# A planned one-core kernel: GpSimd is made to wait for the VectorE instruction listed ahead of it, TensorE's fillers change, the first-stage result gets a second buffer

## The chip, the core and the metric

One core of a Trainium2 chip runs the whole kernel. The metric is the time of one execution in device microseconds (us). The kernel before took 555.62 us, the median of three runs (557.21, 555.62 and 553.38 us).

## What is computed

An input of 2048 tokens by 576 channels goes through two residual blocks. Each block normalises the tokens and applies a scale and a shift that come from a small vector `c`. The first block is a state-space layer (a causal convolution of every channel over all tokens, with taps from 128 complex poles per channel). The second is a gated feed-forward network on the eight tokens with the highest router score; every other token passes unchanged.

```
mod = (silu(c) @ w_mod).reshape(1, 6, 1, 576)          # sa, ca, ga, sb, cb, gb
h = layernorm(x) * (1 + ca) + sa
x = x + ga * A(h)
h = layernorm(x) * (1 + cb) + sb
x = x + gb * B(h)

A: P = exp((A * dt)[:, :, None] * pos);  K = 2 * einsum("dn,dnl->dl", C, P).real
   y = irfft(rfft(h, 2L) * rfft(K, 2L))[:L] + h * D_skip
B: r = h @ w_r;  idx = the 8 tokens with the largest r
   y = (silu(h[idx] @ w_gate) * (h[idx] @ w_up)) @ w_down * sigmoid(r[idx])
   h + scatter(y, idx)
```

## The kernel before, in words

The program runs in four stages, which overlap.

**Preparation.** `mod_row` makes the six modulation rows from 1440 KB pieces of `w_mod` (TensorE, line 626, then line 640). `prep_polar` and `prep_poles` turn the pole parameters into 16-bit pieces on VectorE. `stage1(b)`, for eight pairs of token groups, multiplies the normalised tokens `hb` by a 32-point transform (lines 739 and 742). The result goes from PSUM into two SBUF tiles, `xs0` and `xs1` (line 748), and four DMAs on SyncE's queue write these to `dX` in DRAM (line 754). Both tiles have one buffer: the copies of `stage1(b+1)` wait until the stores of `stage1(b)` have landed.

**Taps and convolution.** For each of 36 blocks of 16 channels, `mags` makes exponentials `E` (ScalarE, line 798), `trig` makes sines and cosines `SC` (ScalarE, lines 828, 830, 832) after a range reduction `n` (VectorE, line 347), and `taps` multiplies them: `SC<-SC,E` on GpSimd, `Bc<-E,SC` and two products `E<-E,SC` on VectorE, one of these on either engine. TensorE contracts the products (line 858); the result goes to `ksb`. `kx` transforms the taps (line 879). When a group of eight blocks is done, `conv` runs eight steps: TensorE (lines 923 and 937), two products `t<-b,us` on VectorE, two sums `t<-t` on GpSimd, the inverse on TensorE (line 971), a DMA through `dZ`, and `y_group` (line 1009).

**The memory that is handed on.** The setup's tiles (tag `su`) must all be done before the convolution's pool `grp` opens (`swap3`). The pool for the feed-forward weights, `w1`, opens when the taps and the fourth group are done (`swap4`), a second one, `w2`, when the fifth is (`swap5`).

**Tail.** Router scores, selection, the feed-forward network on 32 rows, the normalised output (three VectorE passes `zr<-zr` of 1.35 us each per pair of token groups), and the scatter. The weights stream from DRAM in 39 DMAs.

**What sets the order.** No engine's order is written by hand. `Plan` holds 2254 operations with a cost, dependencies, ring buffers and PSUM banks, and lists them by start times of its own; `SEEDS` is a table of numbers that perturbs the priorities and so picks one list. Then `emit` issues the operations in the order of that list, each on its engine's queue. An operation marked `lock` (the GpSimd instructions and the VectorE instructions with two SBUF inputs or in a fast mode) is listed so that no two of them run at once: in the list, GpSimd and VectorE take turns. On the chip nothing enforces these turns. An instruction starts when its data are there and its engine's queue has reached it.

**Fillers.** `spare` counts gaps in TensorE's list, and `idle` puts 128x128 fp32 matmuls of the identity (part of `csm`, a 413 KB constant) into them, at line 438. Their result is not used. A gap gets no more of them than bring the last 3.4 us (`WINDOW`) to a share of 0.8 (`SHARE`). They come after 12 us of the planner's time (`FROM`), and stop from 130 us (`HOLD`) until the PSUM bank that they use is free again.

Of the kernel before, what the change touches and what calls it, by code (L numbers as in the profile page):

```python
# [37 lines left out]
class Plan:  # L38

    LAT = {"V": .12, "A": .17, "P": .12, "T": .21, "Q": 0.0, "X": 0.0}  # L40
    LOOK, TABLE, RATE, FLY, AHEAD = .3, 1.28, 370.0, 2.0, 2.0
    SEEDS = ((15, 0.32), (789, 1), (1215, 0.32), (1311, 0.32), (1887, 0.32), (3271, 0.32), (4311, 0.32), (5223, 0.32), (5319, 0.32), (13159, 0.32), (16055, 0.32), (23663, 0.32), (35487, 0.32), (35511, 0.32), (36455, 0.32), (37575, 0.32), (39311, 0.32), (43039, 0.32), (62487, 0.32), (94159, 0.32), (220535, 0.32), (314815, 0.32), (322255, 0.32), (349359, 0.32), (362815, 0.32))
    wide = False
# [163 lines left out]
    def spare(self):  # L207

        ts = [o for o in self.done if o.on == "T"]
        out, load = {}, []  # L210
        late = max((o.gone for o in self.done if o.need and set(o.names) & set(self.NARROW)), default=0.0)
        for a, b in zip(ts, ts[1:]):
            t0 = a.start + (a.cost["T"] if isinstance(a.cost, dict) else a.cost)
            t1 = b.start
            load.append((a.start, t0))
            while load and load[0][1] < t1 - self.WINDOW:
                load.pop(0)
            full = sum(y - max(x, t1 - self.WINDOW) for x, y in load)
            n = min(int((t1 - t0 - self.GAP) / self.UNIT), math.ceil((self.SHARE * self.WINDOW - full) / self.UNIT))
            if n > 0 and (t1 < self.HOLD or t0 > late) and t0 > self.FROM:  # L220
                out[b] = n
                load.append((t0, t0 + n * self.UNIT))
        return out

    GAP, WINDOW, UNIT, FROM, SHARE, idle = .3, 3.4, .27, 12.0, .8, None

    def emit(self):
        Plan.last = self
        self.done = self.schedule()
        fill = self.spare() if self.idle else {}  # L230
        for o in self.done:
            if o in fill:
                self.idle(fill[o], o.start > self.HOLD)
            if o.need:
                o.fn(o.on, o.names)
            else:
                o.fn(o.on)


# [101 lines left out]
def adaln_s4d_mod_kernel(ctx, tc, u, par0, par1, head, wm, wr, wg, wu, wd, cs, cfg, cmv, out):  # L341
    nc = tc.nc
    V, S, P, T, Q = nc.vector, nc.scalar, nc.gpsimd, nc.tensor, nc.sync
    AX = mybir.AxisListType.X

    def ts(o, a, s1, op0, s2=None, op1=None, eng=None):
        (eng or V).tensor_scalar(o, a, s1, s2, op0=op0, **({"op1": op1} if op1 is not None else {}))  # L347

    def stt(o, a, s, b, op0, op1, **kw):
        V.scalar_tensor_tensor(o, a, s, b, op0=op0, op1=op1, **kw)  # L350

    def tt(o, a, b, op, eng=None):
        (eng or V).tensor_tensor(o, a, b, op=op)  # L353

# [78 lines left out]
    def idle(n, late):  # L433

        if "p" not in IDLE or IDLE["late"] != late:
            IDLE["p"], IDLE["late"] = ps.tile([128, 128], F32, name=plan.NARROW[0]), late
        for _ in range(n):
            T.matmul(IDLE["p"], ident, ident, start=True, stop=True)  # L438
    plan.idle = idle
    CH = ((0, 128), (128, D - 128))  # L440
    PP, PAR = {0: pp}, {0: pp.tile([128, 4, 128], F32, name="par0")}
# [283 lines left out]
    def stage1(b):  # L725
        for m in range(2):
            ring(f"xs{m}", b, 1)
        for j in range(2):
            ln_rows(2 * b + j)
            for hh in range(2):  # L730
# [13 lines left out]
                for m in range(2):  # L744
                    def g(e, j=j, m=m, cs_=cs_, st=st):
                        if (b, m) not in XS:
                            XS[b, m] = su.tile([128, 2, D], F32, name=f"xs{m}")
                        CP[e](XS[b, m][:, 1 - j if m == 0 else j, cs_], st["p"][m])
                    op("AV", {"A": ac(288), "V": vc(288)}, g, uses=[mm], w=[("xsp", b, m, j, hh)], inst=[(f"xs{m}", b)],
                       tag="su")  # L750
        for m in range(2):
            s0 = 14 - 2 * b if m == 0 else 2 * b
            for cc in range(2):
                op("Q", .45, lambda e, m=m, cc=cc, s0=s0: Q.dma_start(
                    dX[cc, m, s0:s0 + 2].rearrange("s h k d -> (h k) s d"), XS[b, m][64 * cc:64 * cc + 64]),
                   r=[("xsp", b, m, j, hh) for j in range(2) for hh in range(2)], inst=[(f"xs{m}", b)],
                   w=[("dX", b, m, cc)], dma=295, tag="su")
# [636 lines left out]
    def cols(e, nm):  # L1394

        stc["p"] = banks([128, 2, 5], nm)[0]
        for i, x in enumerate((cb(), sb())):
            for k in range(5):
                for h in range(2):
                    c = 128 * k + 64 * h if k < 4 else 512  # L1400
                    T.matmul(stc["p"][64 * h:64 * h + 64, i, k:k + 1], x[0:1, c:c + 64], ones[0:1, 0:1],
                             start=True, stop=True, tile_position=(0, 64 * h))
    m_ = op("T", 1.2, cols, r=both("cb") + both("sb"), bank=1, tag="su")
    op("AV", {"A": .2, "V": .12}, lambda e: CP[e](csc, stc["p"]), uses=[m_], w=["csc"], tag="su")
# [69 lines left out]
```

## Time and profile before

| | |
|---|---|
| median of three runs | 555.62 us (553.38 to 557.21) |
| the profiled execution | 557.26 us, span 555.5 us |
| instructions | 17725 |
| busy time: TensorE matmuls, weight loads | 470.0 us (85% of the span), 330.4 us |
| busy time: VectorE, ScalarE, GpSimd | 410.5 us (74%), 322.6 us (58%), 171.7 us (31%) |
| fillers | 255 matmuls, recorded as 510 |
| HBM read, written | 71.88 MB, 23.62 MB |

The span runs from the program's first instruction to its last, and the execution's own time is 1.76 us longer. An fp32 matmul leaves two records. A busy time is a sum over the whole span, so it does not tell which engine bounds a stage; the chain of work that ended last does, step by step. PEclk is the share of the full clock that TensorE was granted.

### The profile page before, as it was taken

The page shows a single profiled execution, that of the slowest core. Times are in us where ns is not written, and L with a number is a line of the kernel's source. Part 1 is how long each engine was busy: PE and PEld are TensorE (multiplying, and loading weights), DVE is VectorE, ACT ScalarE, POOL GpSimd, SP SyncE. Part 2 cuts the span into 40 slices and gives each one's busy share as a digit, 9 for nine tenths or more (in the row PEclk, how much of TensorE's full clock was granted, in tenths as well). Part 3 has the DMA queues.
Part 4 walks back from the last instruction along what each step waited for, and adds up shares of the span by engine and source line. Part 5 has one row for each costly group of instructions (what it writes and reads, how often), then busy time and mean ns, then how long its engine had stood idle before and what let it go on. Part 6 is the DMA issues. An engine that isn't in the chain of part 4 may idle for free.

```text
span 555.5 us, 17725 instructions
## 1 busy us (share of the span) xinstructions
PE 470.0 (85%) x7589; PEld 330.4 (59%) x7589; DVE 410.5 (74%) x861; ACT 322.6 (58%) x529; POOL 171.7 (31%) x135
## 2 busy tenths in 40 slices
PE   3979898788877789999998899888889479989886
PEld 2755454553556556767676567566778366446453
DVE  4699889877644968798978999979877588554501
ACT  5488579656555879778896897876421003421100
POOL 0003124302212656366836465365722000000000
PEclk9999989887778979999999999999999996999988
DMA  8965333204392211373345323153387899899993
GB/s 349 426 274 173 105 98 88 73 25 128 100 322 90 59 40 61 102 184 100 95 126 146 94 81 99 58 153 117 109 238 200 199 295 383 258 280 379 389 320 144
DMA packets 67285, 96.66 MB, mean 174 GB/s; under 512 B 12891, under 2 KB 46811, under 8 KB 66054
## 3 DMA queue, kind: packets, MB, share of 16 engines
q1 hardware_dynamic: 66070, 92.49, 51.4%
q10 hardware_dynamic: 1104, 3.01, 1.4%
q8 instruction: 60, 0.98, 0.8%
q14 instruction: 19, 0.16, 0.1%
q0 software_dynamic: 32, 0.02, 0.0%
HBM read 71.88 MB, written 23.62 MB: 172 GB/s over the span
## 4 chain that ended last, share of the span: by engine, by line
PE 37%; DVE 22%; DMA 17%; issue 10%; ACT 9%; POOL 3%; SPq 2%; POOLq 0%; DVEq 0%; ACTq 0%
DMA out<-zr 6%; PE b L971 6%; PE b L858 4%; PE b L923 4%; PE b L937 4%; DVE zr L353 4%; DVE n L347 4%; DMA w<-in_wu 3%; PE b L739 3%; PE b L879 3%; DVE Bc L353 3%; DVE t L353 3%; ACT E L798 3%; DMA dX<-xs 2%; DVE E L350 2%
## 5 line engine op out<-in xcount | busy, mean ns | idle before, releaser
L353 POOL TENSOR_TENSOR SC<-SC,E 128x1024 f32<-128x1024 f32 x36 | 87.2, 2424 | 132.4 <-ACT SC L832 61.1
L353 POOL TENSOR_TENSOR t<-t 128x256 f32<-128x256 f32 (+1 forms) x80 | 68.7, 863 | 96.2 <-DVE t L353 94.3
L438 PEld LDWEIGHTS b<-csm 128*128 128x128 f32 x510 | 70.1, 210 | 18.8 <-issue 16.4
L438 PE MATMUL b<-csm 128*128 128x128 f32 x510 | 78.0, 303 | 0.0
L798 ACT ACTIVATE E<-b 128x512 f32<-128x512 f32 x108 | 57.8, 608 | 8.1 <-PE b L792 6.9
L353 DVE TENSOR_TENSOR t<-b,us 128x512 f32<-128x512 f32 (+1 forms) x80 | 47.6, 630 | 12.7 <-PE b L937 10.9
L353 DVE TENSOR_TENSOR Bc<-E,SC 128x1024 f32<-128x1024 f32 x36 | 51.9, 1441 | 0.9 <-PE b L858 0.9
L971 PE MATMUL b<-t,fg 64*128 64x128 f32 (+1 forms) x640 | 45.5, 282 | 5.5 <-POOL t L353 3.3
L828 ACT ACTIVATE SC<-ph 128x1024 f32<-128x1024 f32 x36 | 36.9, 1025 | 21.6 <-PE b L858 7.7
L347 DVE TENSOR_SCALAR n<-ph 128x1024 f16<-128x1024 f32 x36 | 43.8, 1216 | 6.7 <-PE ph L809 6.5
L971 PEld LDWEIGHTS b<-t,fg 64*128 64x128 f32 x640 | 39.0, 187 | 13.6 <-issue 5.9
L923 PE MATMUL b<-xu,fg 128*64 128x128 f32 (+1 forms) x640 | 41.9, 276 | 1.9 <-DVE t L353 0.8
L858 PE MATMUL b<-Bc,SC 128*32 128x64 f32 x1152 | 40.0, 236 | 2.8 <-DVE us L928 0.8
L858 PE MATMUL b<-E,SC 128*32 128x64 f32 x1152 | 39.0, 233 | 3.9 <-DVE E L353 2.2
L832 ACT ACTIVATE SC<-SC,halfpi 128x1024 f32<-128x1024 f32 x36 | 41.3, 1147 | 0.1
L923 PEld LDWEIGHTS b<-xu,fg 128*64 128x64 f32 x640 | 34.3, 142 | 11.5 <-issue 4.8
L1242 ACT ACTIVATE zr<-hx,rs 128x576 f32<-128x576 f32 x16 | 12.8, 861 | 48.8 <-DVE rs L350 31.3
L792 PE MATMUL b<-mv,s 128*128 128x512 f16 x108 | 35.0, 394 | 6.6 <-ACT E L798 4.7
L937 PE MATMUL b<-xk,fg 128*64 128x128 f32 (+1 forms) x640 | 39.6, 270 | 0.7 <-ACT E L798 0.2
L1326 POOL DMA_INDIRECT out<-yo,icol x1 | 1.0, 1041 | 126.2 <-DVE yo L353 126.2
L350 DVE SCALAR_TENSOR_TENSOR E<-E,SC 128x512 f32<-128x512 f32 x36 | 36.7, 1019 | 1.0
L937 PEld LDWEIGHTS b<-xk,fg 128*64 128x64 f32 x640 | 32.6, 139 | 7.5 <-issue 1.9
(231 smaller groups left out, 871.5 us busy)
## 6 DMA issues: line engine op xcount, KB each, us to landing
w<-in_wd SPq DMA_DIRECT2D x12, 864.0 KB, 10.0
dX<-xs SPq DMA_DIRECT2D x32, 288.0 KB, 4.1
w<-in_wg SPq DMA_DIRECT2D x12, 768.0 KB, 5.3
w<-in_wu SPq DMA_DIRECT2D x12, 768.0 KB, 9.5
wt<-in_wm SPq DMA_DIRECT2D x6, 1440.0 KB, 14.7
xu<-dX SPq DMA_DIRECT2D x32, 256.0 KB, 3.1
dZ<-zs SPq DMA_DIRECT2D x32, 256.0 KB, 2.3
zr<-dZ SPq DMA_DIRECT2D x64, 128.0 KB, 3.3
```

The lines of the kernel that those rows point to most:

```text
L347: (eng or V).tensor_scalar(o, a, s1, s2, op0=op0, **({"op1": op1} if op1 is not None else {}))
L350: V.scalar_tensor_tensor(o, a, s, b, op0=op0, op1=op1, **kw)
L353: (eng or V).tensor_tensor(o, a, b, op=op)
L438: T.matmul(IDLE["p"], ident, ident, start=True, stop=True)
L792: T.matmul(p, par[b][si], mv[:, i], start=True, stop=True)
L798: S.activation(ES[b][:, h], st["p"], AF.Exp)
L828: S.activation(sc()[:, :, 0], PH[b], AF.Abs)
L832: op("A", ac(1024) + .13, lambda e: S.activation(SCS[b][:, :, 0], SCS[b][:, :, 0], AF.Sin, scale=-TWO_PI, bias=halfpi), w=[("ca", b), ("cb ...
L858: T.matmul(kp[32 * t4:32 * t4 + 32, x], SC[:, 0, ri, 32 * i:32 * i + 32], mo[ri][:, i], start=ri == 0, stop=ri == 1, tile_position=(0, 32 ...
L923: T.matmul(pu[64 * a:64 * a + 64, q, cc], f2[:, 2 * q + a, cc], xu[:, 2 * q + a], start=True, stop=True)
L937: T.matmul(pk[64 * a:64 * a + 64, q, cc], f2[:, 2 * q + a, cc], xk[:, k0 + 2 * q + a], start=True, stop=True)
L971: T.matmul(pz[a][:, q], g2[r, 2 * q + cc], pr[r, q, 1 - cc], start=cc == 0, stop=cc == 1, tile_position=(64 * a, 0))
```

## The change

1. **Turns at the shared port.** After each `lock` operation, `emit` calls `turn`. It remembers VectorE's last instruction, and makes the next GpSimd instruction in the list wait for it. The reverse, VectorE waiting for GpSimd, is not added.
2. **Fillers.** They multiply a constant column of ones, broadcast to 128x128 for both operands, which a VectorE memset makes at the start, and no longer the identity from DRAM. They may come before the first matmul, from 1 us of the planner's time, and up to a share of 0.92 early, 0.8 late.
3. **Two buffers** for `xs0` and for `xs1`.
4. **The issue cost** of a `dX` store in the planner is 0.8 instead of 0.45.
5. **`cols`** (line 1401) does full columns with one matmul of 128 instead of two of 64: 12 matmuls instead of 20.
6. **Another table of seeds**, so another list.

```diff
-    SEEDS = ((15, 0.32), (789, 1), (1215, 0.32), (1311, 0.32), (1887, 0.32), (3271, 0.32), (4311, 0.32), (5223, 0.32), (5319, 0.32), (13159, 0.32), (16055, 0.32), (23663, 0.32), (35487, 0.32), (35511, 0.32), (36455, 0.32), (37575, 0.32), (39311, 0.32), (43039, 0.32), (62487, 0.32), (94159, 0.32), (220535, 0.32), (314815, 0.32), (322255, 0.32), (349359, 0.32), (362815, 0.32))
+    SEEDS = ((5, 1), (55, 0.32), (63, 0.32), (189, 1), (279, 0.32), (335, 0.32), (983, 0.32), (4383, 0.32), (5703, 0.32), (18399, 0.32), (32567, 0.32), (35447, 0.32), (46567, 0.32), (156343, 0.32), (162871, 0.32), (272111, 0.32), (281391, 0.32), (282783, 0.32), (332647, 0.32), (384183, 0.32))
...
-        for a, b in zip(ts, ts[1:]):
-            t0 = a.start + (a.cost["T"] if isinstance(a.cost, dict) else a.cost)
+        for a, b in zip([None] + ts, ts):
+            t0 = a.start + (a.cost["T"] if isinstance(a.cost, dict) else a.cost) if a else self.FROM
             t1 = b.start
-            load.append((a.start, t0))
+            if a:
+                load.append((a.start, t0))
...
-            n = min(int((t1 - t0 - self.GAP) / self.UNIT), math.ceil((self.SHARE * self.WINDOW - full) / self.UNIT))
-            if n > 0 and (t1 < self.HOLD or t0 > late) and t0 > self.FROM:
+            share = self.SHARE[t0 > late]
+            n = min(int((t1 - t0 - self.GAP) / self.UNIT), math.ceil((share * self.WINDOW - full) / self.UNIT))
+            if n > 0 and (t1 < self.HOLD or t0 > late):
...
-    GAP, WINDOW, UNIT, FROM, SHARE, idle = .3, 3.4, .27, 12.0, .8, None
+    GAP, WINDOW, UNIT, FROM, SHARE, idle, turn = .3, 3.4, .27, 1.0, (.92, .8), None, None
...
+            if o.lock and self.turn:
+                held = self.turn(o.on, held)
...
-            T.matmul(IDLE["p"], ident, ident, start=True, stop=True)
+            T.matmul(IDLE["p"], bc(ones, [128, 128]), bc(ones, [128, 128]), start=True, stop=True)
...
+    def turn(on, held):
+
+        if on == "V":
+            return last.get(V)
+        if held is not None and last.get(P) is not None and last[P] is not turned[0]:
+            tc.add_manual_dep(last[P].ins, held.ins.name, mybir.DependencyInfo(mybir.DependencyClass.Sync, mybir.DependencyReason.DATA), reason="port")
+            turned[0] = last[P]
+        return None
+    turned = [None]
+    plan.turn = turn
...
-            ring(f"xs{m}", b, 1)
+            ring(f"xs{m}", b, 2)
...
-                            XS[b, m] = su.tile([128, 2, D], F32, name=f"xs{m}")
+                            XS[b, m] = su.tile([128, 2, D], F32, name=f"xs{m}", bufs=2)
...
-                op("Q", .45, lambda e, m=m, cc=cc, s0=s0: Q.dma_start(
+                op("Q", .8, lambda e, m=m, cc=cc, s0=s0: Q.dma_start(
...
-                for h in range(2):
-                    c = 128 * k + 64 * h if k < 4 else 512
-                    T.matmul(stc["p"][64 * h:64 * h + 64, i, k:k + 1], x[0:1, c:c + 64], ones[0:1, 0:1],
+                for h in range(1 if k < 4 else 2):
+                    c, n = (128 * k, 128) if k < 4 else (512, 64)
+                    T.matmul(stc["p"][64 * h:64 * h + n, i, k:k + 1], x[0:1, c:c + n], ones[0:1, 0:1],
                              start=True, stop=True, tile_position=(0, 64 * h))
-    m_ = op("T", 1.2, cols, r=both("cb") + both("sb"), bank=1, tag="su")
+    m_ = op("T", .7, cols, r=both("cb") + both("sb"), bank=1, tag="su")
```

`last` holds the latest instruction that the helpers `ts`, `stt` and `tt` issued on each engine. The helper of all `TENSOR_TENSOR` instructions is line 353 before and line 359 in the changed kernel.

The list moves everywhere, but each engine still does nearly the same work: GpSimd has 7 of the `E` products instead of 9, ScalarE 39 table loads instead of 41, TensorE 265 fillers instead of 255. Three places matter below.

GpSimd's queue from its first product on, with what each instruction waits for. Before:

```order
L353 TENSOR_TENSOR SC<-SC,E 128x1024 [waits Activation_49] x2
L353 TENSOR_TENSOR SC<-SC,E 128x1024 [waits PE_49,DVE_49,Activation_49,Pool_49] x2
L353 TENSOR_TENSOR E<-E,SC 128x512 [waits DVE_49]
L353 TENSOR_TENSOR SC<-SC,E 128x1024 [waits PE_49,Activation_49,Pool_49]
L353 TENSOR_TENSOR E<-E,SC 128x512 [waits DVE_49]
L353 TENSOR_TENSOR SC<-SC,E 128x1024 [waits PE_49,Activation_49,Pool_49]
```

The same place in the changed kernel:

```order
L359 TENSOR_TENSOR SC<-SC,E 128x1024 [waits DVE_49,Activation_49]
L359 TENSOR_TENSOR E<-E,SC 128x512 [waits DVE_49]
L359 TENSOR_TENSOR SC<-SC,E 128x1024 [waits Activation_49]
L359 TENSOR_TENSOR SC<-SC,E 128x1024 [waits PE_49,DVE_49,Activation_49,Pool_49] x2
L359 TENSOR_TENSOR E<-E,SC 128x512 [waits DVE_49]
L359 TENSOR_TENSOR SC<-SC,E 128x1024 [waits PE_49,DVE_49,Activation_49,Pool_49]
```

The wait `DVE_49` is now on `SC` products that before waited for ScalarE and TensorE alone. The `E` products keep theirs, but it may now name a later VectorE instruction.

TensorE's queue at the start. Before:

```order
L626 MATMUL b_166<-wt,scb 32x144 x20
L590 MATMUL b_198<-dx,ones 128x144 x2
L640 MATMUL b_203<-sm,csm 128x144 x2
L640 MATMUL b_209<-sm,csm 128x144 x2
L590 MATMUL b_216<-dx,ones 128x144 x2
L626 MATMUL b_229<-wt,scb 32x144 x20
L640 MATMUL b_264<-sm,csm 128x144 x2
L640 MATMUL b_268<-sm,csm 128x144 x2
L438 MATMUL b_283<-csm 128x128 x8
```

The changed kernel:

```order
L444 MATMUL b_165<-ones 128x128 x12
L607 MATMUL b_178<-dx,ones 128x144 x2
L607 MATMUL b_187<-dx,ones 128x144 x2
L444 MATMUL b_165<-ones 128x128
L643 MATMUL b_202<-wt,scb 32x144 x20
L657 MATMUL b_244<-sm,csm 128x144 x2
L657 MATMUL b_248<-sm,csm 128x144 x2
L444 MATMUL b_165<-ones 128x128
L643 MATMUL b_255<-wt,scb 32x144 x20
```

Twelve fillers stand ahead of the first real matmul, and single ones between the modulation rows, where before eight stood in one place.

ScalarE's queue where `stage1` reuses the `xs` tiles. Before, from the end of the first pair of token groups (`xs_544`, `xs_546`) to the start of the second (`xs_650`, `xs_693`):

```order
L748 COPY xs_544<-b_549 128x288 [waits PE_49]
L748 COPY xs_546<-b_550 128x288 [waits PE_49]
L748 COPY xs_544<-b_560 128x288 [waits PE_49]
L513 ACTIVATE ay_605<-par_351 128x448
L544 ACTIVATE par_351<-par_351 128x448
L828 ACTIVATE SC<-ph 128x2x512 [waits DVE_49,PE_49,Pool_49]
L863 COPY ksb<-b_570 128x256
L798 ACTIVATE E<-b_635 128x512 [waits PE_49]
L798 ACTIVATE E<-b_644 128x512 [waits PE_49]
L748 COPY xs_650<-b_613 128x288 [waits DMAHW7_49,DMAHW6_49,Activation_49]
L748 COPY xs_650<-b_625 128x288
L748 COPY xs_693<-b_614 128x288 [waits DMAHW1_49,DMAHW0_49,DVE_49]
```

The changed kernel, from the end of the second pair (`xs_828`, `xs_830`) into the third (`xs_1202`, `xs_1204`), the first that reuses a buffer:

```order
L765 COPY xs_830<-b_1155 128x288 [waits PE_49]
L765 COPY xs_828<-b_1163 128x288 [waits PE_49]
L765 COPY xs_828<-b_1173 128x288 [waits PE_49]
L765 COPY xs_1202<-b_1183 128x288 [waits DMAHW7_49,DMAHW6_49,PE_49]
L765 COPY xs_1204<-b_1184 128x288 [waits DMAHW1_49,DMAHW0_49,PE_49]
L765 COPY xs_1202<-b_1194 128x288 [waits PE_49]
L765 COPY xs_1204<-b_1195 128x288 [waits PE_49]
L765 COPY xs_1202<-b_1209 128x288 [waits PE_49]
L765 COPY xs_1204<-b_1210 128x288 [waits PE_49]
L765 COPY xs_1202<-b_1221 128x288 [waits PE_49]
```

The wait for the stores (`DMAHW`) now names those of two pairs earlier, and the second pair has none.

More of the change, by code (lines that the diff above doesn't have):

```diff
@@ L230, in emit @@
         fill = self.spare() if self.idle else {}
+        held = None
         for o in self.done:
@@ L344, in adaln_s4d_mod_kernel @@
     AX = mybir.AxisListType.X
+    last = {}
     def ts(o, a, s1, op0, s2=None, op1=None, eng=None):
-        (eng or V).tensor_scalar(o, a, s1, s2, op0=op0, **({"op1": op1} if op1 is not None else {}))
+        last[eng or V] = (eng or V).tensor_scalar(o, a, s1, s2, op0=op0, **({"op1": op1} if op1 is not None else {}))
     def stt(o, a, s, b, op0, op1, **kw):
-        V.scalar_tensor_tensor(o, a, s, b, op0=op0, op1=op1, **kw)
+        last[V] = V.scalar_tensor_tensor(o, a, s, b, op0=op0, op1=op1, **kw)
     def tt(o, a, b, op, eng=None):
-        (eng or V).tensor_tensor(o, a, b, op=op)
+        last[eng or V] = (eng or V).tensor_tensor(o, a, b, op=op)
     def bc(ap, shape):
```

## The prediction

> **What bounds the kernel now.** First the page's chain of work that ended last, then the busy time by stage. The stages are cut where memory is handed on: preparation, start of the convolution, taps and convolution, last group, tail. The columns are the stretch, its length, the busy times of TensorE's matmuls and weight loads, VectorE, ScalarE and GpSimd, then granted clock, DMA share and GB/s.
>
> ```profile
> PE 37%; DVE 22%; DMA 17%; issue 10%; ACT 9%; POOL 3%; SPq 2%; POOLq 0%; DVEq 0%; ACTq 0%
> ```
> ```profile
> 0.00:156.00 156.00, 128.17 (x1443) 82.73 (x1447) 122.81 (x284) 105.80 (x185) 32.17 (x19) 0.91 0.49 169
> 156.00:200.00 44.00, 33.30 (x732) 23.59 (x720) 26.43 (x36) 27.88 (x45) 16.61 (x12) 0.82 0.38 130
> 200.00:410.00 210.00, 191.33 (x4192) 143.58 (x4192) 181.49 (x305) 165.13 (x258) 116.33 (x91) 1.00 0.38 113
> 410.00:443.00 33.00, 22.60 (x386) 20.40 (x384) 23.21 (x83) 3.59 (x13) 5.56 (x12) 1.00 0.77 205
> 443.00:556.00 113.00, 94.61 (x861) 60.05 (x861) 56.55 (x155) 20.23 (x30) 1.04 (x1) 0.89 0.88 302
> ```
>
> No engine is full before 443 us. The chain changes hands between TensorE and VectorE at nearly every step, so time is lost where one waits at the wrong moment. GpSimd holds 3% of it: slow, but rarely last. The final 113 us move weights and output at 302 GB/s with the DMA engines 88% busy. These transfers wait for memory that the convolution gives back, and the change touches none of them: I let the tail keep its length and move as a block. What the change is worth is then decided before 443 us.
>
> **Term 1: the second buffer.** From the chain, with start, length and holder:
>
> ```profile
> 52.59 0.72 SPq L754
> 53.36 3.47 DMA dX<-xs
> ...
> 59.73 0.57 SPq L754
> 60.34 0.61 SPq L754
> 61.05 0.75 SPq L754
> 61.84 4.15 DMA dX<-xs
> ...
> 125.71 5.64 DMA dX<-xs
> ```
>
> Three stores (13.26 us) and four issues (2.65 us) stand on it, 15.9 us. Each time a copy into `xs` waits for the last store. With two buffers it waits for a store two pairs older, so these pieces go. What is late next is VectorE and ScalarE, which copy the results out and have other work queued. Bounds: a gain of 15.9 us, or 0 if those queues fill the time. In the preparation VectorE has 156 - 122.8 = 33 us without work, twice the wait, so I take half: 8 us.
>
> **Term 2: the turns.** The contended groups (instructions, busy us, mean ns), then VectorE's timeline with two undisturbed instructions and a disturbed one, then GpSimd's beside the latter:
>
> ```profile
> L353 DVE TENSOR_TENSOR Bc<-E,SC 128x1024 f32<-128x1024 f32 x36 | 51.9, 1441 | 0.9 <-PE b L858 0.9
> L350 DVE SCALAR_TENSOR_TENSOR E<-E,SC 128x512 f32<-128x512 f32 x36 | 36.7, 1019 | 1.0
> L353 DVE TENSOR_TENSOR E<-E,SC 128x512 f32<-128x512 f32 x27 | 22.2, 822 | 0.0
> L353 POOL TENSOR_TENSOR SC<-SC,E 128x1024 f32<-128x1024 f32 x36 | 87.2, 2424 | 132.4 <-ACT SC L832 61.1 <-ACT E L798 42.3 <-issue 12.8
> ```
> ```profile
> 286.41 1.22 DVE L353 TENSOR_TENSOR Bc<-E,SC 128x1024 f32<-128x1024 f32 x1
> ...
> 287.66 0.69 DVE L350 SCALAR_TENSOR_TENSOR E<-E,SC 128x512 f32<-128x512 f32 x1
> ...
> 300.71 4.51 DVE L350 SCALAR_TENSOR_TENSOR E<-E,SC 128x512 f32<-128x512 f32 x1
> ```
> ```profile
> 300.41 1.27 POOL L353 TENSOR_TENSOR E<-E,SC 128x512 f32<-128x512 f32 x1
> 301.66 2.34 POOL L353 TENSOR_TENSOR SC<-SC,E 128x1024 f32<-128x1024 f32 x1
> 303.96 0.71 POOL L353 TENSOR_TENSOR t<-t 128x256 f32<-128x256 f32 x1
> ```
>
> GpSimd began 0.3 us before VectorE's `E`, and VectorE then stood through three GpSimd instructions. So the port is held for a whole instruction, and here it was not handed over in between. Over all, with 1.22 and 0.69 us as the undisturbed lengths, VectorE loses 36 x (1.441 - 1.22) = 8.0, 36 x (1.019 - 0.69) = 11.8 and 27 x (0.822 - 0.69) = 3.6 us, 23.4 in all.
>
> Which of it do turns remove? I matched the nth instruction of each kind in the trace with the nth in the planner's list. Of 19 `E` products that lost over 0.15 us, 18 met a GpSimd instruction that stands behind them in the list. Those are the ones that must now wait. Most of the stalled `Bc` met one that stands ahead of them, and those stay. What counts is the part on the chain:
>
> ```profile
> 93.53 1.75 DVE E L350
> 95.28 2.46 DVE ax L347
> ...
> 106.97 2.46 DVE th L347
> ...
> 149.63 1.80 DVE E L350
> ...
> 300.79 2.84 DVE E L350
> ```
>
> Less 0.69 us for each `E`, and about 0.4 for each of the two short fast-mode instructions (the first of them has a sister of 0.40 us, below), that is 1.06 + 2.06 + 2.06 + 1.11 + 2.15 = 8.4 us in the five largest.
>
> ```profile
> 99.44 0.40 DVE L347 TENSOR_SCALAR ax<-ax 128x448 int32<-128x448 int32 x1
> ```
>
> Some smaller ones follow, so the bounds are a gain of about 11 us and none. I take 7, nearer to the upper one: an `E` that ends earlier releases TensorE's contraction of that block directly.
>
> The price: GpSimd is in order, so behind each waiting `SC` stand the sums `t<-t` of the convolution, and TensorE's inverse waits for these. Built without the turns, the same list has a VectorE wait on 8 of the 36 `SC` products; with them on 24, 17 of them new. One that waits for an `E` starts up to 0.69 us later, one that waits for a `Bc` and an `E` 1.91. Bounds: 0, since GpSimd holds 3% of the chain, and 17 x 1.91 = 32 us, if all of it reached the end. The nearest row is GpSimd's share, 3%; I take 3 us of loss.
>
> **Term 3: the fillers.** The chain at the start:
>
> ```profile
> 12.74 2.22 PE b L640 x8
> ...
> 16.21 2.76 PE b L626 x40
> ...
> 21.61 2.71 PE b L438 x16
> 24.32 1.54 PE b L626 x40
> ...
> 26.28 0.76 PE b L640 x4
> ```
>
> The same 40 records take 2.76 us ahead of the eight fillers and 1.54 behind them; TensorE ran cold up to there, which the clock column, 1.00 in the first stage's beginning for lack of records, does not show. A warm start would save at most 1.2 us on each of two modulation rows, 0.7 on each of two steps like the first row (2.22 against 2 x 0.76), and about 1 on the fillers, some 5 us. But the twelve new fillers end early: at 2.71 / 8 = 0.34 us each they are done by about 5 us. The next matmul needs `dx`, which VectorE makes only here:
>
> ```profile
> 9.08 0.74 DVE L353 TENSOR_TENSOR dx<-csm,dta 64x576 f32<-64x576 f32 x1
> ```
>
> TensorE is idle for some 4.7 us in between, and this trace shows what such a gap does (3.4 us with 0.49 us of matmuls, and the next stretch at half clock):
>
> ```profile
> 95.10:98.50 3.40, 0.49 (x5) 0.32 (x4) 3.40 (x3) 2.22 (x4) 2.39 (x1) 1.00 0.59 140
> 98.50:101.90 3.40, 2.97 (x67) 1.97 (x67) 1.95 (x5) 0.00 (x0) 0.00 (x0) 0.50 0.65 212
> ```
>
> The Trainium skill ("TensorE: Matmul & The Clock Gate", Part 1) says that one busy window of about 3.4 us lifts the clock and one idle window drops it. Its second half agrees with these rows; its first does not, since the matmuls from 8.7 to 21.6 us stayed slow. If the first half held behind the gap, the modulation rows would be warm from the second on, a gain of some 3 us that the sum leaves out.
>
> Fillers also cost: the eight above are on the chain with 2.71 us. There are now 265 instead of 255, and the new list has two runs of twelve right before a long row of `stage1`. Bounds: 5 us of gain, and 24 x 0.34 = 8 us of loss, if those two runs find no gap. I take 0.
>
> **Smaller terms.** `cols` stands on the chain:
>
> ```profile
> 141.14 2.23 PE b L1401 x40
> ```
>
> 24 of 40 records remain: 0.9 us at this half clock, 0.5 warm; I take 0.5. The planner's new issue cost does nothing on the chip. Two table loads less on ScalarE I cost at nothing, because ScalarE has 50 us without work in the preparation and 45 in the middle. The other list is the open item: it spreads `stage1` differently, and no row prices it. I take 0, and widen the range.
>
> **The sum.** 557.3 (the profiled execution) - 8 - 7 + 3 - 0.5 = 544.8 us. This execution took 1.6 us more than the median of the runs shown, so the forecast for the median is 543 us.
>
> **The rivals.**
>
> *Everything on the chain pays.* -15.9 - 11 - 5 - 0.9 = -33, 523 us for the median. For it: three separate waits, at separate places. Against it: VectorE has 28 us without work in the 210 us of the middle, and other waits end close behind those removed.
>
> *It is swallowed.* The stores' time goes to VectorE's queue, the turns move the wait from VectorE to GpSimd, and TensorE, fed no earlier, drops its clock elsewhere: 555 us. For it: the clock column reads 0.91 and 0.82 in the first two stages, and a TensorE that ends sooner has longer gaps. Against it: the pieces named are on the chain, not beside it.
>
> *GpSimd's wait turns round, and it is slower.* `SC` of the next block now starts behind the last `E` of this one. VectorE then reaches the next `Bc` while `SC` holds the port, and nothing makes the order better in that direction. Each such meeting costs VectorE up to 2.42 us. The middle's 28.5 us without work and the 15 us of terms 1 and 2 cover 43.5 / 2.42 = 18 of the 36 blocks; from there it is slower, and with 24 blocks it is 555.6 + 6 x 2.42 = 570 us. For it: `Bc` already meets `SC` ahead of it. Against it: the list keeps `Bc` behind `SC` in any case, with other work for VectorE between, and its mean loss is 0.22 us.
>
> *The change doesn't do what it says*: GpSimd's wait names the `E` that it would have met in only part of the cases. Then term 2 is gone, without its price: 543 + 4 = 547 us, inside the forecast.
>
> **How the numbers follow.** Forecast (533 to 550) 0.50, all pays 0.13, swallowed (550 to 561) 0.25, slower 0.12. A quarter of the swallowed lies below 550. A measurement tells about 1% from no change, so: faster by over 1% 0.50 + 0.13 + 0.07 = 0.70, within 1% 0.18, slower 0.12. The range goes from 528, which leaves out the far half of the first rival, to 558.
>
> **What would show it.** Right: `E<-E,SC` at means near 0.7 us, `Bc` near 1.4; no `dX<-xs` on the chain between the pairs; the first `xu<-dX` issue, which marks the end of the preparation, before 148 us instead of 154.9; a tail of still about 113 us.
> ```profile
> L912 SPq DMA_DIRECT2D xu<-dX x40: 359/371/1379, 154.9 to 417.2; - x40
> ```
>
> (The times in that row are from the first issue to the last.) Wrong: `Bc` means above 1.8 us, a GpSimd share of the chain above 6%, or a preparation that still ends at 155 us.

## The result, and the profile after

The changed kernel takes 531.4 us (median of 4 runs, 528.49 to 532.06); the kernel before took 556.4 us beside it. The ratio is 0.954, 95% interval 0.946 to 0.961: 25 us less. The forecast was 543 us in a range of 528 to 558. So the direction and the range held, and the gain is twice the one forecast (543 us would have been 12.6 us below the 555.62 us that were known). The profiled execution of the changed kernel took 531.41 us, its span is 529.6 us.

First the chain of work that ended last, then the busy times by stage, with the same columns as in the prediction. The stages are cut at the same events as before, so their ends have moved.

```profile
PE 39%; DVE 20%; DMA 14%; ACT 12%; issue 9%; SPq 3%; POOL 2%; ACTq 1%; POOLq 0%; DVEq 0%
```
```profile
0.00:134.00 134.00, 113.73 (x1338) 75.77 (x1339) 114.18 (x280) 97.84 (x172) 26.06 (x18) 0.96 0.55 194
134.00:178.00 44.00, 35.32 (x843) 26.88 (x842) 27.55 (x42) 31.28 (x57) 14.98 (x12) 0.84 0.43 144
178.00:377.00 199.00, 185.84 (x4079) 137.56 (x4080) 170.99 (x282) 163.21 (x251) 101.13 (x87) 0.98 0.37 107
377.00:414.00 37.00, 30.34 (x478) 27.00 (x473) 26.80 (x97) 4.30 (x15) 7.12 (x17) 0.91 0.84 254
414.00:530.00 116.00, 94.14 (x868) 59.94 (x866) 59.29 (x170) 19.70 (x29) 1.04 (x1) 0.91 0.86 288
```

VectorE has less of the chain (20 for 22%), DMA less (14 for 17%), GpSimd 2 for 3%. Three milestones divide the time more sharply: the first issue of `xu<-dX` ends the preparation, the first issue of `w<-in_wg` opens the tail. The row of `xu` before is in the prediction. Here is its sister for `w` before, and both after (the two times are the first and the last issue):

```profile
L1052 SPq DMA_DIRECT2D w<-in_wg x12: 328/454/667, 403.4 to 513.9; - x12
```
```profile
L929 SPq DMA_DIRECT2D xu<-dX x40: 360/371/1232, 134.1 to 390.0; - x40
L1069 SPq DMA_DIRECT2D w<-in_wg x12: 328/476/627, 377.2 to 486.7; - x12
```

| stretch, us | before | after |
|---|---|---|
| preparation (0 to the first `xu`) | 154.9 | 134.1 |
| middle (to the first `w`) | 248.5 | 243.1 |
| tail (to the span's end) | 152.1 | 152.4 |

The tail moved as a block. Of 25.9 us of span, 20.8 came from the preparation. One store is still on the chain, although the prediction's sign of being right was that none would be:

```profile
110.93 3.78 DMA dX<-xs
```

So the second buffer does not cover every wait in the new list, which puts the `dX` stores closer together (issued from 64.9 to 130.1 us, before from 50.0 to 150.7).

The groups that contend for the port, with instructions, busy us and mean ns:

```profile
L359 POOL TENSOR_TENSOR SC<-SC,E 128x1024 f32<-128x1024 f32 x36 | 85.0, 2362 | 137.3 <-ACT SC L849 37.1 <-DVE bs L702 34.7 <-ACT xs L765 23.3
L359 DVE TENSOR_TENSOR Bc<-E,SC 128x1024 f32<-128x1024 f32 x36 | 53.4, 1484 | 4.9 <-PE b L875 4.0 <-ACT SC L849 0.9
L359 POOL TENSOR_TENSOR t<-t 128x256 f32<-128x256 f32 x64 | 47.2, 746 | 77.7 <-DVE t L359 43.7 <-DVE E L359 21.3 <-DVE ksb L359 5.7
L356 DVE SCALAR_TENSOR_TENSOR E<-E,SC 128x512 f32<-128x512 f32 x36 | 25.9, 718 | 1.4
L359 DVE TENSOR_TENSOR E<-E,SC 128x512 f32<-128x512 f32 x29 | 19.8, 684 | 0.0
```

`E` fell from 1019 and 822 ns to 718 and 684, `Bc` stayed (1441, 1484): most of the meetings with an instruction listed behind are gone, those of `Bc` remain. New is the releaser `DVE E L359` before the sums `t<-t`, 21.3 us. GpSimd's sums gained too; before, they were

```profile
L353 POOL TENSOR_TENSOR t<-t 128x256 f32<-128x256 f32 x64 | 61.3, 961 | 79.5 <-DVE t L353 77.7
```

Where a turn is taken, VectorE's and GpSimd's timelines in the changed kernel read so:

```profile
299.71 0.68 DVE L356 SCALAR_TENSOR_TENSOR E<-E,SC 128x512 f32<-128x512 f32 x1
300.31 0.69 DVE L359 TENSOR_TENSOR E<-E,SC 128x512 f32<-128x512 f32 x1
```
```profile
301.14 2.23 POOL L359 TENSOR_TENSOR t<-t 128x256 f32<-128x256 f32 x3 [1.61 <-DVE E L359]
303.33 2.35 POOL L359 TENSOR_TENSOR SC<-SC,E 128x1024 f32<-128x1024 f32 x1
```

GpSimd stands for 1.61 us until the second `E` is done, then runs sums and `SC` at their undisturbed lengths. Before, an `E` in such a place took 4.51 us.

### The profile page after: what moved, and what is told of

It is laid out like the page before. It is cut to its first block, busy times and chain, and to the rows that moved or that the text cites. A ratio compares the mean times of both kernels' runs of the same rounds, so it can differ in the third digit from the quotient of the medians.

```text
span 529.6 us, 17735 instructions
## 1 busy us (share of the span) xinstructions
PE 459.4 (87%) x7593; PEld 327.1 (62%) x7593; DVE 398.8 (75%) x867; ACT 316.3 (60%) x523; POOL 150.3 (28%) x133
## 4 chain that ended last, share of the span: by engine, by line
PE 39%; DVE 20%; DMA 14%; ACT 12%; issue 9%; SPq 3%; POOL 2%; ACTq 1%; POOLq 0%; DVEq 0%
PE b L875 5%; PE b L988 5%; PE b L940 5%; DMA out<-zr 4%; PE b L954 4%; PE b L756 4%; DMA w<-in_wg 3%; PE b L896 3%; DVE n L353 3%; ACT E L815 3%; DVE zr L359 3%; PE ph L836 2%; PE ph L826 2%; DVE Bc L359 2%; PE b L809 2%
## 5 line engine op out<-in xcount | busy, mean ns | idle before, releaser
L359 POOL TENSOR_TENSOR SC<-SC,E 128x1024 f32<-128x1024 f32 x36 | 85.0, 2362 | 137.3 <-ACT SC L849 37.1
L444 PEld LDWEIGHTS b<-ones 128*128 128x128 f32 x530 | 73.5, 210 | 19.9 <-issue 16.5
L444 PE MATMUL b<-ones 128*128 128x128 f32 x530 | 82.3, 302 | 1.0 <-DVE ones L435 1.0
L359 POOL TENSOR_TENSOR t<-t 128x256 f32<-128x256 f32 (+1 forms) x80 | 54.1, 687 | 94.7 <-DVE t L359 60.6
L359 DVE TENSOR_TENSOR Bc<-E,SC 128x1024 f32<-128x1024 f32 x36 | 53.4, 1484 | 4.9 <-PE b L875 4.0
L359 DVE TENSOR_TENSOR t<-b,us 128x512 f32<-128x512 f32 (+1 forms) x80 | 46.9, 630 | 10.7 <-PE b L954 6.4
L845 ACT ACTIVATE SC<-ph 128x1024 f32<-128x1024 f32 x36 | 36.9, 1025 | 18.7 <-PE b L875 8.3
L875 PE MATMUL b<-Bc,SC 128*32 128x64 f32 x1152 | 37.7, 227 | 9.0 <-issue 5.2
L940 PEld LDWEIGHTS b<-xu,fg 128*64 128x64 f32 x640 | 33.2, 141 | 11.7 <-issue 3.9
L875 PEld LDWEIGHTS b<-Bc,SC 128*32 128x32 f32 x1152 | 27.9, 112 | 18.3 <-issue 14.6
L847 ACT ACTIVATE SC<-ph 128x1024 f32<-128x1024 f32 x36 | 36.7, 1020 | 0.2
L875 PE MATMUL b<-E,SC 128*32 128x64 f32 x1152 | 36.8, 225 | 0.0
```

What stands on the lines that cost most here:

```text
L359: last[eng or V] = (eng or V).tensor_tensor(o, a, b, op=op)
L444: T.matmul(IDLE["p"], bc(ones, [128, 128]), bc(ones, [128, 128]), start=True, stop=True)
L845: S.activation(sc()[:, :, 0], PH[b], AF.Abs)
L847: op("A", ac(1024), lambda e: S.activation(sc()[:, :, 1], PH[b], AF.Sin, scale=TWO_PI), r=[("ph", b)], w=[("sa", b), ("sb", b)], inst=[("S ...
L875: T.matmul(kp[32 * t4:32 * t4 + 32, x], SC[:, 0, ri, 32 * i:32 * i + 32], mo[ri][:, i], start=ri == 0, stop=ri == 1, tile_position=(0, 32 ...
L940: T.matmul(pu[64 * a:64 * a + 64, q, cc], f2[:, 2 * q + a, cc], xu[:, 2 * q + a], start=True, stop=True)
```

## The experiments

The theory at the outset: since most of the gain lies in the preparation, the other list, the second buffer and a warmer clock bring it, and the turns bring some 5 us in the middle. Each run is given as its ratio to the kernel before, on the same chip, with the interval. Differences in us are 1 minus that ratio, times the kernel before's median in the same comparison (552.4 to 553.2 us). The milestones come from one profile each; two profiles of like kernels differ by some us there (243.1 and 248.5 in the middle for two kernels that have no turns and the same list), so the ratios decide.

**The changed kernel, less one part.**

```diff
-    plan.turn = turn
+    plan.turn = None
```

> The changed kernel, same list, GpSimd's added waits taken out. Milestones of the changed kernel: first xu issue 134.1 us, first weight issue 377.2, end 529.6. Theory 1 (the gain is in the preparation: other list, second buffer, warmer clock; the turns bring about 5 us in the middle): the E products go back to means near 1.0 us, first xu issue stays at 134 +- 2, the middle grows from 243 to 247-250, the time is 535-539. Theory 2 (the turns carry half or more of the 25 us, in the preparation too): first xu issue after 138, time 543-548. Theory 3 (turns only move the wait to GpSimd): 530-533.

544.4 us, ratio 0.986 (0.980 to 0.993). Its milestones:

```profile
L929 SPq DMA_DIRECT2D xu<-dX x40: 359/371/1565, 142.0 to 404.6; - x40
L1069 SPq DMA_DIRECT2D w<-in_wg x12: 328/436/1701, 390.6 to 502.1; - x12
```

The preparation is 7.9 us longer than with turns, the middle 5.5. Theory 2 holds and the first theory falls: the turns are at least half of the gain (0.986 against 0.954 for the whole change, and 0.960 for the next kernel on this chip), and they work in the preparation too.

```diff
-            T.matmul(IDLE["p"], bc(ones, [128, 128]), bc(ones, [128, 128]), start=True, stop=True)
+            T.matmul(IDLE["p"], ident, ident, start=True, stop=True)
...
-    GAP, WINDOW, UNIT, FROM, SHARE, idle, turn = .3, 3.4, .27, 1.0, (.92, .8), None, None
+    GAP, WINDOW, UNIT, FROM, SHARE, idle, turn = .3, 3.4, .27, 12.0, .8, None, None
```

(The loop that places the fillers went back as well.)

> The changed kernel, same list, with the fillers of before (128x128 of the identity, none ahead of the planner's 12 us, share .8). Theory 1a (a warm TensorE in the preparation is a large part of the gain): clock records of half speed come back for 15-40 us of the preparation, first xu issue 140-146, time 538-544. Theory 1b (the list and the buffer carry it, fillers only fill): first xu issue 134-137, time 531-535, as the recorded forecast had it with 0 for this term.

530.0 us, ratio 0.960 (0.954 to 0.967); first `xu` at 134.7 us. The fillers bring nothing that can be measured here. Theory 1a falls.

```diff
-                            XS[b, m] = su.tile([128, 2, D], F32, name=f"xs{m}", bufs=2)
+                            XS[b, m] = su.tile([128, 2, D], F32, name=f"xs{m}")
```

> The changed kernel, the same list planned for two buffers, with only one buffer of xs in memory. Theory 1a/1b (the second buffer removes a wait that the new list would meet): dX<-xs is back on the chain three times or more, 10-16 us, first xu issue 144-150, time 541-548. Rival (the list alone carries the gain, the wait falls into the queues' other work): first xu issue below 139, time 532-537.

570.6 us, ratio 1.033 (1.026 to 1.040): slower than the kernel before. The first and the last of seven stores on its chain, and its longest wait of this kind (waiting instruction, releaser, us in all, times, longest):

```profile
66.99 4.09 DMA dX<-xs
...
158.61 3.85 DMA dX<-xs
```
```profile
ACT xs L765 <- DMA dX<-xs: 29.9, 10, 4.6
```

The first `xu` comes at 176.1 us, far later than either theory had it. The new list puts the stores of `stage1` closer together (64.9 to 130.1 us with two buffers), and a single buffer then makes one pair after another wait for a store. So the buffer cannot be judged without the list that uses it.

The next one is built from the other side: the kernel before, with its planner's costs, rings and seeds and so its list, and on it the turns, the second buffer, the new fillers and the merged matmuls of `cols`. Against the changed kernel the edit is:

```diff
-            ring(f"xs{m}", b, 2)
+            ring(f"xs{m}", b, 1)
...
-                op("Q", .8, lambda e, m=m, cc=cc, s0=s0: Q.dma_start(
+                op("Q", .45, lambda e, m=m, cc=cc, s0=s0: Q.dma_start(
...
-    m_ = op("T", .7, cols, r=both("cb") + both("sb"), bank=1, tag="su")
+    m_ = op("T", 1.2, cols, r=both("cb") + both("sb"), bank=1, tag="su")
```

and the seeds of before.

> All parts of the change (turns, second buffer, new fillers, merged cols) on the list of before: costs, rings and seeds of the planner are those of before, so only the order of the list is undone. Theory 1b (the new order carries most): first xu issue 146-150, time 541-548. Rival (the parts carry it whatever the list): first xu issue 133-139, time 529-535. My recorded forecast priced just this kernel, at 543.

533.5 us, ratio 0.967 (0.962 to 0.973), first `xu` at 135.0. The old list with all parts gives most of the gain. What the list brings by itself is not settled: against the new list with the old fillers (530.0, on the same chip) it is 3.5 us and the intervals overlap, against the changed kernel's own ratio (0.954, measured apart) 7 us and they don't. Theory 1b falls and the rival holds: the parts carry most of the gain.

**The kernel before, plus one part.** The list is that of before in all four.

```diff
+            if o.lock and self.turn:
+                held = self.turn(o.on, held)
```

(with `turn` itself and the helpers' `last`, as in the change)

> The kernel before with the turns alone; its list, one buffer, its fillers. Milestones of before: first xu issue 154.9 us, first weight issue 403.4, end 555.5. Theory 1 (the parts add up; the turns take 13 us, 8 in the preparation and 5 in the middle, as they did on the changed kernel): first xu issue 146-148, middle 243, time 11-15 us below the kernel before, about 540. Rival (the turns pay only once the buffer is there, because the wait for the store swallows them in the preparation): first xu issue 152-155, only the middle gains, 4-7 us below, about 547. The recorded forecast: 4 us below.

539.5 us, ratio 0.977 (0.971 to 0.983): 12.7 us less, 9 to 16 by the interval.

```profile
L930 SPq DMA_DIRECT2D xu<-dX x40: 359/371/1865, 147.6 to 401.9; - x40
L1070 SPq DMA_DIRECT2D w<-in_wg x12: 328/465/872, 388.9 to 497.7; - x12
```

The preparation is 7.3 us shorter, although ScalarE and VectorE still wait 10.2 us for stores, and the middle (241.3) 7.2. The turns don't need the buffer. A warmer clock doesn't explain it: at a granted clock of 0.94 over the whole run the kernel before took 553.2 us and this one 542.0 (clock 0.941), at 0.96 it was 547.7 (0.959) and 540.3 (0.961).

```diff
-                            XS[b, m] = su.tile([128, 2, D], F32, name=f"xs{m}")
+                            XS[b, m] = su.tile([128, 2, D], F32, name=f"xs{m}", bufs=2)
```

> The kernel before with a second buffer for xs in memory, everything else as before, the list too. Theory 1 (the parts add up): the three stores leave the chain, first xu issue 142-145, middle unchanged at 248, time 10-13 us below the kernel before, about 542. Rival (the freed time is taken by VectorE's stalls as long as there are no turns): first xu issue 148-152, 3-6 us below. The recorded forecast: 8 us below, about 545.

543.9 us, ratio 0.986 (0.980 to 0.992): 7.8 us less, 5 to 11.

```profile
L912 SPq DMA_DIRECT2D xu<-dX x40: 359/371/1162, 145.3 to 406.5; - x40
L1052 SPq DMA_DIRECT2D w<-in_wg x12: 328/442/1177, 392.5 to 505.1; - x12
```

The preparation is 9.6 us shorter, the middle (247.2) about as it was. That is less than the 10 to 13 us expected, and what the recorded forecast had. No store is left on the chain, so of its 15.9 us some 8 to 10 came back. The chain now runs through VectorE instead: in the preparation its pieces add up to 60.7 us, before to 36.9.

```diff
-    GAP, WINDOW, UNIT, FROM, SHARE, idle = .3, 3.4, .27, 12.0, .8, None
+    GAP, WINDOW, UNIT, FROM, SHARE, idle = .3, 3.4, .27, 1.0, (.92, .8), None
...
-            T.matmul(IDLE["p"], ident, ident, start=True, stop=True)
+            T.matmul(IDLE["p"], bc(ones, [128, 128]), bc(ones, [128, 128]), start=True, stop=True)
```

> The kernel before with the new fillers alone; same list. Theory 1b: as on the changed kernel they bring nothing beyond 0.5%, 550-556, first xu issue 153-156. Rival (on the kernel before, whose preparation ran at half clock for 50 us, they do count): half-clock records before the first xu issue fall below 25 us, first xu issue 147-151, time 545-549.

550.7 us, ratio 0.997 (0.993 to 1.001), first `xu` at 153.2: no difference that can be told.

The second buffer together with the turns:

```diff
-                            XS[b, m] = su.tile([128, 2, D], F32, name=f"xs{m}")
+                            XS[b, m] = su.tile([128, 2, D], F32, name=f"xs{m}", bufs=2)
```

> The kernel before with turns and second buffer, without new fillers, merged cols and new list. Theory 1 (these two carry all of the gain): first xu issue 134-137, middle 242, time 528-534, the same as with all parts on the old list (533.5). Rival (fillers or cols are needed to hold the clock): above 538.

532.0 us, ratio 0.961 (0.955 to 0.967): 21.5 us less, where the two alone gave 12.7 + 7.8 = 20.5. They add up within the intervals, and together they are the change but for some 4 us (0.961 against 0.954) that the intervals don't separate.

**What in the turns counts.**

Four variants of `turn`, the first three on the kernel before, the last on the changed kernel. `last["op"]` is the operation of GpSimd's last instruction: products multiply, sums add or subtract.

```diff
-        if held is not None and last.get(P) is not None and last[P] is not turned[0]:
+        if held is not None and last.get(P) is not None and last[P] is not turned[0] and last["op"] == OP.mult:
```

> The kernel before with turns for GpSimd's products alone (SC and its share of E); the sums t<-t of the convolution don't wait. In the trace of before the stalls on the chain that met a product add up to about 11 us (E 1.07, 1.11, 2.15, 2.17; hb 1.01; the short fast-mode instructions 2.06 and 2.06), those that met a sum to 3 us (seven of 0.4 to 0.5 us). Theory 1 (the stalls on the chain come back in full): 9-11 us below the kernel before, first xu issue 147-149, middle 244-247. Rival (the ladder of Bc, sum, E in the middle and GpSimd's own lost time of 18 us count most): 4-7 us below, middle 247-249.

544.1 us, ratio 0.989 (0.983 to 0.996): 5.9 us less (2 to 10); first `xu` at 148.4, middle 244.2. The 9 to 11 us of theory 1 were not reached by the median; the rival's 4 to 7 fit.

```diff
-        if held is not None and last.get(P) is not None and last[P] is not turned[0]:
+        if held is not None and last.get(P) is not None and last[P] is not turned[0] and last["op"] != OP.mult:
```

> The kernel before with turns for the sums t<-t alone; the products don't wait. Theory 1: 2-4 us below the kernel before, preparation unchanged (no sums there), middle 244-247. Rival (GpSimd's own lost time counts): 6-9 us below, middle 240-242.

549.5 us, ratio 0.999 (0.995 to 1.003). Alone the sums' turns bring nothing that can be told. That is the more striking as they removed most of GpSimd's stalls. Busy time that went, against before, beside the time gained:

| kernel | VectorE, us | GpSimd, us | gain, us |
|---|---|---|---|
| before + turns | 13.3 | 18.2 | 12.7 (9 to 16) |
| before + products' turns | 8.2 | 2.8 | 5.9 (2 to 10) |
| before + sums' turns | 6.1 | 14.1 | 0.6 (-2 to 3) |

So GpSimd's own lost time, the rival here, paid nothing that can be told. The two halves give 6.5 us by their sum, both together 12.7; the intervals of the halves reach 10 and 3 us, so they just allow simple addition. The halves are not a clean division either: in the list of before, 15 of the 36 `SC` stand behind a sum with no VectorE port instruction between the two. With all turns that sum waits, and they come behind it; with the products' turns alone nothing holds them. How much of the gap this explains stays open.

```diff
         if on == "V":
-            return last.get(V)
+            return None
+        held = last.get(V)
```

> The kernel before with the turns made stricter: a GpSimd product or sum waits for the last VectorE instruction ahead of it in the list, of whatever kind, not only for one that has the port right ahead of it. It takes away few further meetings and adds waits: twice the suspected price. Theory 1 (GpSimd has slack, a wait costs nothing): 538-541, as with the turns alone (539.5). Rival (a wait has a price; the recorded forecast took 3 us for 17 waits on SC, with a bound of 32): 542 or more, GpSimd's share of the chain above 4%.

565.4 us, ratio 1.027 (1.021 to 1.034): slower than the kernel before by 15 us, and 28 slower than with the turns proper (0.977). Its groups and its milestones:

```profile
L360 POOL TENSOR_TENSOR SC<-SC,E 128x1024 f32<-128x1024 f32 x36 | 85.9, 2386 | 119.3 <-DVE n L354 55.0 <-DVE hb L357 41.3 <-ACT xs L767 12.6
L360 DVE TENSOR_TENSOR Bc<-E,SC 128x1024 f32<-128x1024 f32 x36 | 73.4, 2039 | 2.9 <-PE b L877 2.9
```
```profile
L931 SPq DMA_DIRECT2D xu<-dX x40: 359/371/1414, 152.2 to 419.8; - x40
...
L1071 SPq DMA_DIRECT2D w<-in_wg x12: 328/440/604, 406.9 to 515.5; - x12
```

`SC` now waits for `n<-ph`, 55 us in all. That instruction doesn't contend for the port: its mean is 1.22 us before and here, its undisturbed length. `SC` starts later, and VectorE reaches `Bc` while `SC` runs (at 285.61 us an `SC` of 2.37 us starts, at 286.64 a `Bc`, which takes 2.42): `Bc` has a mean of 2.04 us, 36 x (2.04 - 1.22) = 29.5 us lost, where it was 8.0 before. The middle grows to 406.9 - 152.2 = 254.7 us. This is the prediction's rival of the wait that turns round, with its mechanism and its sign. So a wait can have a high price: it had one where GpSimd waited for VectorE's last instruction of whatever kind, and not where it waited only for one that has the port right ahead of it in the list.

```diff
-        if on == "V":
-            return last.get(V)
...
+        me = V if on == "V" else P
+        i = last.get(me)
+        if i is None or turned.get(me) is i:
+            return held
+        turned[me] = i
+        if held is not None and held[0] is not me:
+            tc.add_manual_dep(i.ins, held[1].ins.name, mybir.DependencyInfo(mybir.DependencyClass.Sync, mybir.DependencyReason.DATA), reason="port")
+        return me, i
```

> The changed kernel with turns in both directions: VectorE's port instructions too wait for the GpSimd instruction that has the port ahead of them in the list. This asks what the remaining stalls of Bc (mean 1.48 us against 1.22) are worth. Theory 1 (a stall and a wait of the same length cost the same): 528-533, the same as the changed kernel, Bc means near 1.22 with the lost time as waits ahead of it. Rival a (order alone pays, as for E): below 526. Rival b (VectorE now waits where it used to come first): above 536.

529.1 us, ratio 0.963 (0.958 to 0.968): the same as the changed kernel.

```profile
L359 POOL TENSOR_TENSOR SC<-SC,E 128x1024 f32<-128x1024 f32 x36 | 85.0, 2362 | 134.6 <-DVE bs L703 34.7 <-ACT SC L850 28.3 <-ACT xs L766 22.9
L359 DVE TENSOR_TENSOR Bc<-E,SC 128x1024 f32<-128x1024 f32 x36 | 44.2, 1227 | 16.8 <-POOL SC L359 11.0 <-PE b L876 3.4 <-ACT SC L850 1.1
```

`Bc` is at 1227 ns, and 11.0 us of waiting for `SC` stand ahead of it instead: a stall became a wait of about the same length. Order pays where the wrong instruction went first; where the right one did, it changes only the name of the loss.

All of them side by side; the ratio decides, the stretches (us) are those of one profile each:

| kernel | ratio, interval | preparation | middle | tail |
|---|---|---|---|---|
| before | 1 | 154.9 | 248.5 | 152.1 |
| before + turns | 0.977 (0.971 to 0.983) | 147.6 | 241.3 | 149.6 |
| before + buffer | 0.986 (0.980 to 0.992) | 145.3 | 247.2 | 153.8 |
| before + fillers | 0.997 (0.993 to 1.001) | 153.2 | 243.1 | 155.1 |
| before + turns + buffer | 0.961 (0.955 to 0.967) | 135.5 | 241.5 | 153.1 |
| before + products' turns | 0.989 (0.983 to 0.996) | 148.4 | 244.2 | 151.9 |
| before + sums' turns | 0.999 (0.995 to 1.003) | 150.5 | 241.7 | 152.5 |
| before + strict waits | 1.027 (1.021 to 1.034) | 152.2 | 254.7 | 151.5 |
| all parts on the old list | 0.967 (0.962 to 0.973) | 135.0 | 241.6 | 155.8 |
| changed | 0.954 (0.946 to 0.961) | 134.1 | 243.1 | 152.4 |
| changed, no turns | 0.986 (0.980 to 0.993) | 142.0 | 248.6 | 152.0 |
| changed, old fillers | 0.960 (0.954 to 0.967) | 134.7 | 242.8 | 148.4 |
| changed, one buffer | 1.033 (1.026 to 1.040) | 176.1 | 241.0 | 152.0 |
| changed, turns both ways | 0.963 (0.958 to 0.968) | 134.3 | 239.0 | 151.3 |

## Why the prediction was right in direction and half the size

**The bound** held: the tail kept its length (152.1 and 152.4 us), and everything was decided ahead of it.

**Term 1, the buffer:** taken 8 us, measured 7.8. The reason given (half of the 15.9 us, because VectorE and ScalarE are late next) holds for VectorE: the preparation is 9.6 us shorter, nothing else changes, and VectorE has 24 us more of the chain there, ScalarE no more than before. On the new list one store stayed on the chain (3.78 us).

**Term 2, the turns:** taken 7 us of gain and 3 of price, net 4; measured 12.7 (9 to 16). This is the step that failed, by 9 us: the mechanism was right, and the stalls on the chain that turns can remove were sized too small. The prediction listed five, 8.4 us, bounded all by 11 and took 7. Two things were left out. The smaller ones, at "some smaller ones follow", are these in the chain before:

```profile
103.97 2.47 DVE hb L350 x2
...
192.38 1.10 DVE E L350
193.48 1.13 DVE E L353
...
253.15 1.10 DVE E L350
254.25 1.15 DVE E L353
...
344.81 1.10 DVE E L350
```

`hb` takes 0.81 us undisturbed (in the changed kernel's trace), `E` 0.69, so these are 0.85 + 5 pieces of 0.41 to 0.46 = 3.0 us. The `E` come in a row: `Bc`, then `E` and `E` behind a sum of GpSimd's that slipped between. The other omission is a reading of the chain: it lists part of a stalled instruction as "issue". The `E` at 300.71 us that took 4.51 us stands there with 2.84 us and this piece behind it; another has most of its stall so, here from the chain and from VectorE's timeline:

```profile
303.63 1.52 issue
...
374.36 0.73 DVE E L353
375.09 1.96 issue
```
```profile
374.27 2.85 DVE L353 TENSOR_TENSOR E<-E,SC 128x512 f32<-128x512 f32 x1
```

In both cases the next piece is VectorE's `n`, whose input was ready (TensorE's `ph` ended at 300.82 and 373.73 us), so the chain stood for the `E`. That adds 1.5 and 0.73 + 1.96 - 0.69 = 2.0 us, and two small ones of the same kind (at 266.64 and 324.22) some 0.7. Together it is 8.4 + 3.0 + 4.2 = 15.6 us on the chain, not 11. The measured 12.7 is about four fifths of that (by its interval, three fifths to all); that every piece came back is not shown, and the two halves of the turns, with 6.5 us, speak against a simple rule.

The price of the waits, taken at 3 us, was not measured by itself: between 15.6 and 12.7 there is room for it, and the interval also allows none. The engines' busy times, before and with the turns alone, and `Bc` in the latter:

```profile
PE 470.0 (85%) x7589; PEld 330.4 (59%) x7589; DVE 410.5 (74%) x861; ACT 322.6 (58%) x529; POOL 171.7 (31%) x135
```
```profile
PE 459.7 (85%) x7589; PEld 322.2 (60%) x7589; DVE 397.2 (74%) x861; ACT 322.3 (60%) x529; POOL 153.5 (29%) x135
...
L360 DVE TENSOR_TENSOR Bc<-E,SC 128x1024 f32<-128x1024 f32 x36 | 54.1, 1504 | 1.8 <-PE b L876 1.8
```

GpSimd's busy time fell by 18.2 us, so it stands for a semaphore where it stood for the port. `Bc`, which the waits could have pushed into `SC`, went from 1441 to 1504 ns, 2.3 us over all 36. A price that shows exists only for the strict waits.

**Term 3, the fillers:** taken 0, measured a gain of 1.8 us with an interval across 0. The step inside it held too: the clock was granted to the twelve early fillers (14 records up to 4.09 us took 3.13 us, the 12 of the first row below 1.30) and dropped in the gap ahead of `dx`. The changed kernel's windows:

```profile
4.09:7.51 3.42, 1.30 (x12) 1.10 (x10) 3.04 (x20) 3.37 (x6) 0.00 (x0) 1.00 1.05 438
7.51:10.92 3.41, 1.88 (x8) 1.88 (x8) 2.82 (x10) 0.83 (x4) 0.00 (x0) 0.50 1.02 432
10.92:14.33 3.41, 3.41 (x44) 2.14 (x43) 3.24 (x16) 1.69 (x7) 0.00 (x0) 0.50 1.00 422
14.33:17.74 3.41, 3.00 (x58) 2.32 (x50) 1.46 (x3) 2.42 (x5) 0.00 (x0) 1.00 0.98 413
```

(The windows are cut where the clock records change.) One window full of matmuls, 10.92 to 14.33, was followed by full clock. By the Trainium skill ("TensorE: Matmul & The Clock Gate", Part 1) one busy window suffices, and these rows agree. Those of the kernel with the new fillers alone do not:

```profile
9.82:13.23 3.41, 3.41 (x19) 2.78 (x12) 1.83 (x9) 1.20 (x5) 0.00 (x0) 0.50 1.05 437
13.23:16.65 3.42, 3.42 (x39) 2.50 (x37) 2.11 (x9) 2.07 (x8) 0.00 (x0) 0.50 0.98 415
16.65:20.06 3.41, 3.01 (x24) 2.18 (x17) 1.50 (x4) 1.87 (x3) 0.00 (x0) 0.50 1.02 418
```

After two full windows the third is still at half clock. What makes the difference between the two kernels stays open.

**Smaller terms.** `cols` was taken at a gain of 0.5 us for 16 records fewer. It lost: on the chain it went from 2.23 to 2.37 us. Two kernels, without and with the merging, each with its window (the granted clock is the third number from the end):

```profile
123.92 1.33 PE L1419 MATMUL b<-ones,m 1*64 1x1 f32 x40 [0.47 <-ACT s L797]
```
```profile
123.90:125.30 1.40, 1.38 (x41) 1.35 (x42) 1.40 (x3) 0.57 (x3) 0.85 (x1) 1.00 0.95 306
```
```profile
128.87 2.44 PE L1418 MATMUL b<-ones,m 1*128 1x1 f32 x24
```
```profile
128.80:131.40 2.60, 2.60 (x28) 2.43 (x26) 0.80 (x3) 2.60 (x4) 0.00 (x0) 1.00 0.95 253
```

Forty records on alternating halves of 64 columns take 1.33 us, 24 of which 16 span 128 columns 2.44. The Trainium skill ("TensorE: Matmul & The Clock Gate", Part 3) says that small matmuls at different tile positions overlap in the array, and these rows are in line with that; the prediction did not weigh it. The row of before, 2.23 us, was at half clock (granted 0.50): a time per record taken from it and carried to another shape was the error.

**The list:** taken 0, and it brings 0 to some 7 us. But on it the second buffer is worth 44 us (1.033 against 0.954), where it was 7.8 on the list of before, which the prediction did not see: the list and the buffer belong together.

**The rivals.** *All pays* (523) holds in part: the turns paid about its 11 us, the buffer half of its 15.9, the fillers nothing that can be told. *Swallowed* is refuted: the two parts that paid gave together what they gave alone. *The wait turns round* did not happen here and was made to happen with strict waits.

## What to carry to other kernels

Where two engines share a port, go through the chain of waits and add up the loss of every instruction on it: the small repeated ones too, and the part of a stalled instruction that the chain lists as "issue". Here 12.7 us of some 15.6 came back. Stalls of the engine that is off the chain are no measure: 14.1 us less of GpSimd's brought nothing that can be told. A wait that makes the slower engine come after the one that has the port ahead of it in the list cost less here than it brought; one that named the last instruction of whatever kind moved the collision elsewhere. And price an edit that merges small instructions by a row of the merged shape, at the same clock.

## What was not expected of the hardware

At full clock (granted 1.00), small matmuls that alternate between two halves of 64 columns took 33 ns a record (1.33 us for 40); with two thirds of them over 128 columns it was three times that (2.44 us for 24, 102 ns). And a stall on the port cost what a wait costs, where it could be compared: with both directions ordered, 9.5 us of `Bc` stalls (36 x 0.26) became 11.0 us of waits, at the same time within 1%.
